# Groups 2 and 3 of the attention output by seven block products, summed up in DRAM

## The chip, the cores and the metric

The kernel runs on one core of a Trainium2 chip. The metric is device time in microseconds of one launch: 727.54 us, the median of three runs (727.34 to 727.63). The profiled execution took 727.55 us, of which its trace spans 725.8 us; 1.75 us lie around the span.

## The reference

Two branches of one input `x` (2048 tokens by 640), mixed by a gate. All of it is float32.

```python
def _A_ref(x, wqkv, wo):                       # 32 heads of 20
    q, k, v = ...                              # x @ wqkv
    pq, pk = phi(q), phi(k)                    # where(t > 0, t + 1, exp(t)) + 1e-6
    kv = einsum("bhsd,bhse->bhde", pk, v)
    z = einsum("bhsd->bhd", pk)
    num, den = einsum("bhqd,bhde->bhqe", pq, kv), einsum("bhqd,bhd->bhq", pq, z) + 1e-6
    return (num / den) @ wo
def _B_ref(x, w_gate, w_up, w_down):
    return (sigmoid(x @ w_gate) * (x @ w_up)) @ w_down
g = sigmoid((x * gate_w).sum(-1))
return g * _A_ref(x) + (1 - g) * _B_ref(x)
```

## The kernel before

Everything is kept transposed, with features in the 128 partitions and tokens in the free dimension. The 640 features are five rows of 128 (`KC`, index k for inputs, o for outputs), the 2048 tokens four groups of 512 (`TG`, index g), the 1536 hidden features of B twelve blocks f.

**Stages.** First k, v and `kv`, then `M`, which is `kv` times `wo`, so that A's last part is one 640 by 640 matrix `M` times p, where p is phi(q). Then q and B for groups 2 and 3 (`f_phase(1, ...)`), then q and B for groups 0 and 1 (`f_phase(0, ...)`, called the f phase below), and the last stage: for each group `out = M (p * fac) + (1 - g) B`, where `fac` is the gate over the denominator. B of groups 2 and 3, already times `1 - g`, waits in `b_dram`; p waits in `p_dram`; `M` is made in DRAM (`m_dram`) and kept there as high and low halves (`mp_dram`). B of groups 0 and 1 is in the SBUF tile `tb`.

**Products.** A float32 product is made of three matmuls in the format float32r, of high and low halves (`mm3`, lines 407 to 409): high by high, high by low, low by high. `split` makes the halves: ACT copies the high one (line 420), DVE subtracts it to get the low one (line 424). One term of one output tile of 128 by 512 is therefore three matmuls.

**Seven products.** Most stages replace the eight products of a 2 by 2 block matrix product by seven (`Block`, steps `s1` to `s7`), with forms S (sums of blocks of the weights) and T (sums of blocks of the inputs) that must be made and split first. Before the change the last stage did so for groups 0 and 1 (`ABlock`: rows 0 and 1, rows 2 and 3 of the output; the fifth input row k = 4 and the fifth output row o = 4 are added plainly by `a_unit`). Groups 2 and 3 were done plainly: ten output tiles of five terms, `a_start` for the first two (line 2611) and `a_unit` for the others. B was put into PSUM ahead of the products (`seed_b`), and each tile went from PSUM to `out_t`.

**What sets the order.** The program is written out by a planner, class `Order`. It keeps estimated clocks for TensorE, ACT and DVE; work that nothing forces yet waits in lists (`urgent`, `items`, `lazy`, `chain`, `spare`) and `fill` places an item as soon as it fits into the slack behind TensorE and its data is thought to have arrived. `need(key)` forces an item. Hooks such as `(FC - 1, 4)` run something after step 4 of block f = 11. Each engine then runs its instructions strictly in the order written.

**Queues and buffers.** Loads go through SP's queue, stores and adding transfers (`accum_op`) through POOL's (GpSimd's). Each queue uses eight semaphores in turn, so a transfer is not issued before the one eight places ahead of it has landed. Tiles come from rotating pools: `ct` gives five buffers of 128 by 512 (`c`), `tt` four (`t`), `x2_tile` ten of twice that size, `h_tile` the `hf` tiles. A tile's next user waits for the last reader of the one before, a transfer too.

In the f phase, `queue_dens` makes `fac` for two groups at a time (five loads of p, ten operations, three small turns through DRAM), and `load_form` and `load_wf` fetch the weights of the blocks ahead: `wg`, `wu`, `ws` (plain and S forms of gate and up), `wf` (those of down).

Of the kernel before, what the change touches and what calls it, by code (L numbers as in the profile page):

```python
# [374 lines left out]
def gated_mix_kernel(ctx: ExitStack, tc: tile.TileContext, xt, xn, wk, wv, wo, wst_q, wst_f, out_t):  # L375
# [1048 lines left out]

    def queue_dens(*gs2):
# [20 lines left out]
        def turn_in(g):  # L1446
            for j in range(4):
                js = slice(j * H, (j + 1) * H)
                sp.dma_start(fac[js, g].rearrange("h (d c) -> h d c", c=P),
                                  den_dram[:, g, j * P:(j + 1) * P].rearrange("(d h) c -> h d c", h=H))  # L1450
            st[g, "gs"] = tt("gs")[:, :P]
            sp.dma_start(st[g, "gs"], gate_rep[4 * g:4 * g + 4].rearrange("i h c -> (i h) c"))
            st["at", g, KC + 1] = lambda: max(order.when(fac[:, g]), order.when(st[g, "gs"])) + 2.5
# [12 lines left out]
        def turn_out(g):  # L1466
            for d in range(4):
                sp.dma_start(fac[d * H:(d + 1) * H, g].rearrange("h (j c) -> h j c", c=P),
                                  fac_dram[:, g].rearrange("(j h) c -> h j c", h=H))
        order.add(0, 0, lambda: [load(g, u) for u in range(2) for g in gs2], chain=True)  # L1470
# [3 lines left out]
        for n, (v, fn) in enumerate(((0, turn_in), (2.0, factor), (0, turn_out))):  # L1474
            for g in gs2:
                order.add(0, v, lambda g=g, fn=fn: fn(g), ("fac", g) if n == 2 else None,
                          lambda g=g, n=n: st.get(("at", g, KC + n), lambda: 1e9)(), **{"first" if n else "chain": True})
# [238 lines left out]
    def queue_m(u=0):  # L1716
# [4 lines left out]
        def fn():  # L1721
# [3 lines left out]
            def rest():  # L1725
                gp.dma_start(mp_dram[:, u], f32(t))
                if u + 1 < KC:
                    queue_m(u + 1)
            order.then(rest)
        order.add(a_cost(D), v_cost(D), fn, "m", lambda: order.when(raw) + 2, spare=True)  # L1730

# [160 lines left out]
    def down_pair(pr, p):  # L1892
# [26 lines left out]
        def far(key, o, g):  # L1919
# [3 lines left out]
            elif not far_at:  # L1923
                far_at.extend(down_pool[1].tile([P, D], F32, name="far", tag=n) for n in ("mr", "mv"))
                far_at.append(down_pool[1].tile([P, TG], F32, name="far", tag="far"))
# [210 lines left out]
    dens = ({3: (2, 3), 7: (0, 1)}, {})  # L2136
# [11 lines left out]
    def f_phase(pr, q, hooks={}):  # L2148
# [70 lines left out]
        for f in range(FC):  # L2219
            if f % 2:  # L2220
                order.need(("h", f // 2 - 1, "B22"), False)
            down = iter(())
            if f in dens[pr]:
                queue_dens(*dens[pr][f])
            if f % 2 and f > 1:
                if pr:
                    pass
                elif f == FC - 1:
                    while any(it[3] == "m" for it in order.spare) or order.pend:
                        order.need("m")  # L2230
                        order._flush()
# [159 lines left out]
    def load_p(g):  # L2391

        PL[g], PL[g, "t"] = [], []
        for u in range(0, KC, 2):
            t = (x2_tile if g == groups[1] else h_tile)(dt=F32)
# [5 lines left out]

    def load_b(g):

        if g < 2:
            BL[g] = [tb[:, o, g] for o in range(KC)]
        elif g == groups[0]:
            BL[g] = [ct("bl") for _ in range(KC)]
            for o in range(KC):
                sp.dma_start(BL[g][o], b_dram[:, o, g - 2])
        else:  # L2410
            t = [x3_tile("bl") for _ in range(2)]
            sp.dma_start(t[0], b_dram[:, 0:3, g - 2])
            sp.dma_start(t[1][:, 0:2], b_dram[:, 3:5, g - 2])
            BL[g] = [t[o // 3][:, o % 3] for o in range(KC)]
# [11 lines left out]
    def pq_tiles(g):  # L2426
# [8 lines left out]
        elif groups.index(g) % 2 == 0:  # L2435
            t = [x2_tile("pq", F32R) for _ in range(5)]
            PQ[g, "t"] = [t[0:3:2], t[1:4:2]]
        else:
            t2 = [x2_tile("pq", F32R) for _ in range(2)]
            t3 = [x3_tile("pq", F32R) for _ in range(2)]  # L2440
            PQ[g] = [tuple(t[:, u] for t in t2) for u in range(2)] + [tuple(t[:, u] for t in t3) for u in range(3)]
            return
# [29 lines left out]
    PT, MS, MR = {}, {}, {}  # L2472

    def load_ms(i):

        if i == 0:
            t = f32(down_pool[1].tile([P, 2, D], F32R, name="mt", tag="mt"))
            raw = [t[:, j] for j in range(2)]
        else:
            raw = [down_pool[1].tile([P, D], F32, name=n, tag=n) for n in ("mr", "mv")]  # L2480
        for j in range(2):
            c0 = (2 * i + j) * P
            m_rows(raw[j].rearrange("p (k c) -> p k c", c=P), slice(c0, c0 + P), gp if i else sp)
        MR[i] = raw, lambda: max(order.when(t) for t in raw)

    def queue_ms(i):

        raw, at = MR.pop(i)
        w = 2 * P
        g, v = raw  # L2490
        a11, a12, a21, a22 = g[:, :w], g[:, w:2 * w], v[:, :w], v[:, w:2 * w]
        g5, v5 = g[:, 2 * w:], v[:, 2 * w:]

        def sums(part):
            if part == 0:
                add(a22, a21, a22)
                sub(a21, a11, a21)
            else:
                sub(a11, a22, a11)
                sub(a12, a12, a11)  # L2500
                sub(g5, g5, v5)

        def form(n, src):
            if i not in MS:
                t = ws_tile() if i == 0 else None
                MS[i] = [t[:, c] for c in range(2)] if t is not None else \
                    [wg_tile().rearrange("p a b -> p (a b)")[:, :9 * P] for _ in range(2)]
            h, l = (t[:, n * w:n * w + width(src)] for t in MS[i])
            split(h, l, src)
        for part in range(2):  # L2510
            order.add(0, 2 * v_cost(w), lambda part=part: sums(part), None, at)
        for n, t in enumerate((a22, a11, a21, a12, g5)):
            order.add(a_cost(width(t)), v_cost(width(t)), lambda n=n, t=t: form(n, t), ("ms", i))

    def queue_pt():
# [5 lines left out]
        def form(t):  # L2521
            if t == 1:
                f = [[down_pool[2].tile([P, TG], F32R, name="pt", tag="c2", bufs=4) for _ in range(2)]
                     for _ in range(2)]
                PT[t] = f
# [4 lines left out]
            PT[t] = [[u[:, j] for u in f] for j in range(2)]  # L2530
# [23 lines left out]
    def a_fifth():  # L2554
# [5 lines left out]
        (2, 7): [queue_m],  # L2560
# [5 lines left out]
        (FC - 1, 4): [lambda: load_ms(0), a_first],  # L2566
# [4 lines left out]
    def next_p():  # L2571
        load_p(groups[1])
        for g in groups[:2]:
            load_b(g)
    last_pair(0, tail, next_p)
    for u in range(KC):
        order.need(("ph", u))
    queue_lo()
    load_ms(1)
    pq_tiles(groups[1])  # L2580
    queue_scale(groups[1])
    queue_pq(groups[1])
    load_p(groups[2])
    load_p(groups[3])

    SEED = {}
    TAGS = ("cc", "ch", "dd", "rot", "rot", "dd", "cc", "ch", "rot", "dd", "cc")

    def seed_b(g, o, tag):

        SEED[g, o] = ps = ps_tile(tag)
        if g < 2:
            vec2(ps, BL[g][o], OMG[g], OP.mult)
        else:
            act(ps, BL[g][o], AF.Copy)

    def queue_seed(g, o, tag, first=True):
        order.add(*((0, v_cost(TG)) if g < 2 else (a_cost(TG), 0)), lambda: seed_b(g, o, tag), ("b", g, o), lambda: BL[g, "at"](), first=first)

    def a_start(units):  # L2600

        ps = [ps_tile(tag) for _, _, tag in units]

        def terms(i, j, first):
            for n, (g, o, _) in enumerate(units):
                os_ = slice(o * P, (o + 1) * P)
                for k in range(KC):
                    l, r = MHL[k, i][:, os_], PQ[g][k][j]
                    if j and n == 0:
                        order.need(("pl", k))  # L2610
                    nc.tensor.matmul(ps[n], l, r, start=first and k == 0, stop=j == 1 and k == KC - 1, skip_group_check=True)  # L2611
                    order.mm(ps[n], TG, first and k == 0, l, r)
                order.fill()
                if j:
                    order.need(("b", g, o))
# [193 lines left out]
```

## Time and profile before

| | |
|---|---|
| median of three runs | 727.54 us |
| profiled execution, its span | 727.55 us, 725.8 us |
| TensorE busy | 721.5 us, 3557 matmuls |
| DVE busy, ACT busy, POOL busy | 573.7 us, 369.0 us, 101.2 us |
| DMA | 182.99 MB, 252 GB/s over the span |
| last stage, from its first matmul to the last operation | 656.69 to 725.8 us |

Matmuls are pipelined: each row of the timeline shows 0.39 us, but the next one starts 0.23 us later. So a sum of TensorE time is made from starts, not from durations. Times in the timeline count from the start of the span. PE in a row is TensorE, SPq is SP issuing a transfer.

### The profile page before, as it was taken

The page shows a single profiled execution, that of the slowest core. Times are in us where ns is not written, and L with a number is a line of the kernel's source. Part 1 is how long each engine was busy: PE and PEld are TensorE (multiplying, and loading weights), DVE is VectorE, ACT ScalarE, POOL GpSimd, SP SyncE. Part 2 cuts the span into 40 slices and gives each one's busy share as a digit, 9 for nine tenths or more (in the row PEclk, how much of TensorE's full clock was granted, in tenths as well). Part 3 has the DMA queues.
Part 4 walks back from the last instruction along what each step waited for, and adds up shares of the span by engine and source line. Part 5 has one row for each costly group of instructions (what it writes and reads, how often), then busy time and mean ns, then how long its engine had stood idle before and what let it go on. Part 6 is the DMA issues. An engine that isn't in the chain of part 4 may idle for free.

```text
span 725.8 us, 10201 instructions
## 1 busy us (share of the span) xinstructions
PE 721.5 (99%) x3557; PEld 619.8 (85%) x3557; DVE 573.7 (79%) x1008; ACT 369.0 (51%) x686; POOL 101.2 (14%) x165
## 2 busy tenths in 40 slices
PE   9999999999999999999999999999999999999998
PEld 8999999988888888888888888888888888888886
DVE  6898878988687889898989954447685868698896
ACT  6884749357656653535454763454333232453551
POOL 0211112113212211211210133000000000012000
PEclk9999999999999999999999999999999999999999
DMA  7676679598787866566787889879979694969612
GB/s 263 156 236 175 178 199 281 134 337 304 262 313 260 330 234 232 180 224 253 254 321 268 245 322 385 322 235 307 327 226 357 207 344 139 359 218 286 249 61 102
DMA packets 79114, 182.99 MB, mean 252 GB/s; under 512 B 12202, under 2 KB 38970, under 8 KB 75478
## 3 DMA queue, kind: packets, MB, share of 16 engines
q1 hardware_dynamic: 60838, 116.94, 49.8%
q0 software_dynamic: 18080, 65.23, 25.8%
q8 instruction: 28, 0.46, 0.3%
q14 instruction: 24, 0.20, 0.1%
q10 hardware_dynamic: 144, 0.16, 0.1%
HBM read 108.68 MB, written 67.07 MB: 242 GB/s over the span
## 4 chain that ended last, share of the span: by engine, by line
PE 99%; DVE 0%; issue 0%
PE ch L407 11%; PE ch L408 11%; PE ch L409 11%; PE cc L407 9%; PE cc L408 9%; PE cc L409 9%; PE dd L407 7%; PE dd L408 7%; PE dd L409 7%; PE rot L408 5%; PE rot L407 5%; PE rot L409 5%; PE rot L1549 1%; PE rot L495 0%; PE ch L2611 0%; PE cc L2611 0%
## 5 line engine op out<-in xcount | busy, mean ns | idle before, releaser
L420 ACT ACTIVATE c<-ch 128x512 f32<-128x512 f32 x52 | 31.1, 598 | 84.0 <-PE ch L409 83.8
L424 DVE TENSOR_TENSOR hf<-c,hf 128x512 fp32r<-128x512 f32 x80 | 54.4, 686 | 22.9 <-ACT hf L420 22.5
L420 ACT ACTIVATE hf<-c 128x512 fp32r<-128x512 f32 x80 | 49.0, 625 | 29.3 <-DVE c L424 29.1
L424 DVE TENSOR_TENSOR c<-cc,c 128x512 f32<-128x512 f32 x40 | 27.6, 689 | 39.0 <-PE cc L409 23.5
L407 PE MATMUL ch<-xth,ws 128*128 128x512 f32 x112 | 43.7, 390 | 0.0
L409 PE MATMUL ch<-xth,ws 128*128 128x512 f32 x112 | 43.6, 389 | 0.0
L408 PE MATMUL ch<-xtl,ws 128*128 128x512 f32 x112 | 43.6, 389 | 0.0
L424 DVE TENSOR_TENSOR tb<-rot,tb 128x512 f32<-128x512 f32 (+1 forms) x58 | 37.0, 672 | 2.8 <-PE rot L409 2.8
L424 DVE TENSOR_TENSOR c<-c,c 128x512 f32<-128x512 f32 x52 | 35.7, 687 | 3.3 <-ACT c L420 2.7
L420 ACT ACTIVATE c<-dd 128x512 f32<-128x512 f32 x22 | 13.1, 597 | 43.5 <-PE dd L409 43.5
L407 PE MATMUL dd<-xrh,wg 128*128 128x512 f32 x90 | 35.2, 391 | 0.0
L409 PE MATMUL dd<-xrh,wg 128*128 128x512 f32 x90 | 35.0, 389 | 0.0
L408 PE MATMUL dd<-xrl,wg 128*128 128x512 f32 x90 | 35.0, 389 | 0.0
L407 PE MATMUL cc<-xbh,ws 128*128 128x512 f32 x84 | 32.7, 389 | 0.0
L408 PE MATMUL cc<-xbl,ws 128*128 128x512 f32 x84 | 32.7, 389 | 0.0
L409 PE MATMUL cc<-xbh,ws 128*128 128x512 f32 x84 | 32.7, 389 | 0.0
L424 DVE TENSOR_TENSOR tb<-dd,tb 128x512 f32<-128x512 f32 x36 | 24.7, 686 | 8.5 <-PE dd L409 8.4
L420 ACT ACTIVATE dd<-ch 128x512 f32<-128x512 f32 x22 | 12.8, 582 | 33.7 <-PE ch L409 33.7
L424 DVE TENSOR_TENSOR wst<-wst 128x256 f32<-128x256 f32 (+1 forms) x65 | 24.6, 396 | 1.4
L424 DVE TENSOR_TENSOR tb<-cc,tb 128x512 f32<-128x512 f32 x36 | 24.4, 683 | 1.2 <-PE cc L409 1.2
L409 PEld LDWEIGHTS ch<-xth,ws 128*128 128x128 f32 x112 | 21.0, 188 | 4.7 <-DVE ws L424 0.2
L420 ACT ACTIVATE c<-c 128x512 f32<-128x512 f32 x34 | 21.3, 628 | 6.9 <-DVE c L424 6.4
(664 smaller groups left out, 2363.5 us busy)
## 6 DMA issues: line engine op xcount, KB each, us to landing
wf<-ws POOLq DMA_DIRECT2D x12, 1152.0 KB, 7.4
ws<-wf SPq DMA_DIRECT2D x11, 1152.0 KB, 8.0
wst<-wst_f SPq DMA_DIRECT2D x12, 640.0 KB, 5.0
wf<-wg POOLq DMA_DIRECT2D x12, 640.0 KB, 6.4
wd<-wd POOLq DMA_DIRECT2D x12, 640.0 KB, 7.9
wg<-wf SPq DMA_DIRECT2D x12, 640.0 KB, 5.6
wf<-wd SPq DMA_DIRECT2D x10, 640.0 KB, 9.5
xnst<-xn SPq DMA_DIRECT2D x16, 320.0 KB, 4.5
```

The source lines that it names most:

```text
L407: nc.tensor.matmul(out, l_hi, r_hi, start=first, stop=False, skip_group_check=True)
L408: nc.tensor.matmul(out, l_hi, r_lo, start=False, stop=False, skip_group_check=True)
L409: nc.tensor.matmul(out, l_lo, r_hi, start=False, stop=last, skip_group_check=True)
L420: nc.scalar.activation(out, src, fn, **kw)
L424: nc.vector.tensor_tensor(out, a, b, op=op)
L1549: nc.tensor.matmul(ps[:w, :w], v[:, m, :w], gt[:, m, c0:c0 + w], start=(m == 0), stop=(m == KC - 1))
```

## The change

Groups 2 and 3 are now done in seven products too.

- The S forms of `M` are made in the f phase for both blocks (`queue_msf`, behind `queue_m`, now from block 3 on), split and stored to a new `ms_dram`; the last stage loads them and makes none.
- The T forms of groups 2 and 3 are made in the f phase without the split (`queue_tp`): p is loaded again, scaled by `fac`, subtracted and stored to a new `pt_dram`. For that all four `fac` are made early (`dens` at blocks 2 and 3, before 3 and 7). The last stage loads and splits the sums (`load_pt`, `queue_form`), and loads three of the five rows of p for group 3 (`load_p3`).
- `a_start` does the products of group 2 that share its p: for both blocks the first two terms and the last three, and the fifth output row. Class `First` does steps 3, 4, 5, 7, 6 for the two blocks alternately; `a_fifth_row` does the fifth row of group 3 on top of what `a_start` left.
- The results aren't seeded with B. Each is summed in a `c` tile and added by POOL's queue into `b_dram`, where B is (`accumulate`). In the last block of products, five transfers bring groups 2 and 3 from `b_dram` to `out_t`.
- The loads of p for group 2 (`load_p0`) come later: after steps 3, 6 and 7 of block 10, before after step 4 of block 9 and steps 3 and 7 of block 10.

```diff
-    dens = ({3: (2, 3), 7: (0, 1)}, {})
+    dens = ({2: (2, 3), 3: (0, 1)}, {})
...
+    def queue_tp(j):
+        src = ((2, j), (2, 2 + j), (3, j), (3, 2 + j))
...
+        def total(n):
+            b11, b21, b12, b22 = raw
+            out, a, b, m = ((b11, b12, b11, 0), (b12, b22, b12, 2), (b22, b22, b11, 1), (b21, b21, b22, 3))[n]
+            sub(out, a, b)
+            gp.dma_start(pt_dram[:, m, j], out)
...
         (FC - 2, 2): [lambda: load_wd(FC - 2)],
-        (FC - 3, 4): [lambda: load_p0(0, 2)],
-        (FC - 2, 3): [lambda: load_p0(2, 4)],
+        (FC - 2, 3): [lambda: order.need('tp'), lambda: load_p0(0, 2)],
+        (FC - 2, 6): [lambda: load_p0(2, 4)],
...
+    def accumulate(g, o, t):
+        gp.dma_start(b_dram[:, o, g - 2], t, accum_op=OP.add)
+
+    def a_start(blks):
...
+        d0, fifth, d1, rest = (ps_tile(t) for t in ("ch", "ch", "dd", "dd"))
+        first, later = range(2), range(2, KC)
+        parts = [(blk.ch, blk.m, first) for blk in blks]
+        parts += [(d0, blks[0].m, later), (fifth, w, first), (d1, blks[1].m, later), (rest, w, later)]
...
+                if n in (0, 1, 3):
+                    out[n] = ct("c11")
+                    act(out[n], ps, AF.Copy, "p")
+                else:
+                    g, o = ((0, 0), (1, 2), (3, 4))[(2, 4, 5).index(n)]
+                    add(out[g], ps, out[g], "p")
+                    accumulate(2, o, out[g])
...
+    class First(ABlock):
...
+        def s4(self):
+            order.need(("pf", 0))
+            order.need(("pq", 3, 4))
+            self.cc = ps_tile("rot")
+            prod(self.cc, self.xt(2, 0, 0) + [self.xb(1, 2, 4)], True)
+            self.c22 = ct("c22")
+            act(self.c22, self.cc, AF.Copy, "p")
+
+        def s5(self):
+            order.need(("pf", 2))
+            prod(self.ch, self.xt(2, 4, 2), False)
+            add(self.c22, self.ch, self.c22, "p")
+            accumulate(3, self.o[1], self.c22)
+
+        def s7(self):
+            for k in range(2, 4):
+                order.need(("pq", 3, k))
+            prod(self.cc, [self.xb(2, 6 + j, 2 + j) for j in range(2)] + [self.xb(2, 8, 4)], False)
+            add(self.c12, self.cc, self.c12, "p")
+            accumulate(3, self.o[0], self.c12)
...
+        if (i, s) == (0, 3):
+            for o in range(KC):
+                sp.dma_start(out_t[o * P:(o + 1) * P, 2 * TG:], b_dram[:, o].rearrange("p g c -> p (g c)"))
```

What this does to the written order, at three places.

**TensorE, the start of the last stage.** `cc`, `ch`, `dd` are PSUM tiles, `pq` the halves of p, `ws` and `wf` those of `M`. Before:

```order
L2611 MATMUL cc_6354<-pq,wf 128x512 x3
L2611 MATMUL ch_6355<-pq,ws 128x512 x2
L2611 MATMUL ch_6355<-pq,wf 128x512 x3
L2611 MATMUL cc_6354<-pq,ws 128x512
L2611 MATMUL cc_6354<-pq,wf 128x512 x4
L2611 MATMUL ch_6355<-pq,ws 128x512
```

Now:

```order
L2700 MATMUL cc_6426<-pq,ws 128x512 x3
L2700 MATMUL cc_6426<-pq,wf 128x512
L2700 MATMUL cc_6427<-pq,ws 128x512 x3
L2700 MATMUL cc_6427<-pq,wf 128x512
L2700 MATMUL ch_6428<-pq,wf 128x512 x6
L2700 MATMUL ch_6429<-pq,ws 128x512 x3
L2700 MATMUL ch_6429<-pq,wf 128x512
L2700 MATMUL dd_6430<-pq,wf 128x512 x6
L2700 MATMUL dd_6431<-pq,wf 128x512 x6
```

The first eight matmuls use rows 0 and 1 of p, the next six (`ch_6428`) rows 2, 3 and 4, two matmuls each. The high halves are used in 30 matmuls, the low ones in the 15 that follow. In all there are 138 matmuls up to `a_unit(0, 4)`, the plain fifth row of group 0, where there were 150.

**ACT, the middle of the last stage**, in the changed program (`c` is a `ct` tile, `rot_6533` and `rot_6547` the products of step 4, `p` the halves of p for group 3, `pt` the fourth T form, `pq` the halves for groups 1 and 0):

```order
L420 ACTIVATE c_6511<-cc_6426 128x512
L420 ACTIVATE p_6304<-hf 128x512
L420 ACTIVATE c_6524<-cc_6427 128x512
L420 ACTIVATE p_6304<-hf 128x512
L420 ACTIVATE c_6543<-rot_6533 128x512
L420 ACTIVATE pt<-pt 128x512 x2
L420 ACTIVATE c_6557<-rot_6547 128x512
L420 ACTIVATE c_6618<-cc_6426 128x512
L420 ACTIVATE pq<-hf 128x512 x3
L420 ACTIVATE c_6635<-cc_6427 128x512
```

Before, ACT put B into PSUM and copied results out of it here, between copies of p. `c_6543` is the eighth tile taken from the five buffers of `ct` (the two `far` tiles are the first two); it gets the buffer of the third, `c_6478`, the first result of `a_start`, and so waits until that one's adding transfer has landed. On DVE the two subtractions for the `pt` copies behind it are the first of 18 operations (the others scale rows of p of groups 0 and 1, add up four results and put B into two PSUM tiles); after these come ten low halves, five of group 1 and then five of group 0.

**SP, the loads for block 9.** Before (`pden` are the rows of p for `fac`):

```order
L364 DMA pden<-p_dram 128x512 x9
L364 DMA wu<-wf_3521 128x768
L364 DMA pden<-p_dram 128x512
L364 DMA wg<-wf_3706 128x1280
L364 DMA ws<-wf_3596 128x2304
L364 DMA wf<-wd_3475 128x2x640 x2
L364 DMA wf<-wd_3475 128x2x1024
```

Now (`mr` and `mv` are the columns of `M` for the first S forms, the `pt` rows those of p for the first T sums):

```order
L364 DMA pt<-p_dram 128x512 x4
L364 DMA wu<-wf_3523 128x768
L364 DMA wg<-wf_3708 128x1280
L364 DMA mr<-m_dram 32x5x128 x4
L364 DMA mv<-m_dram 32x5x128 x4
L364 DMA ws<-wf_3598 128x2304
L364 DMA wf<-wd_3477 128x2x640 x2
L364 DMA wf<-wd_3477 128x2x1024
```

Ten loads of p are gone from here (all `fac` are now made from blocks 2 and 3 on), four others came, and eight transfers of `M`'s columns stand between `wg` and `ws`. The same eight, for the second S forms, stand ahead of `ws` and `wf` of block 11.

More of the change, by code (lines that the diff above doesn't have):

```diff
@@ L2470, in finish @@
         sp.dma_start(out_t[o * P:(o + 1) * P, g * TG + c0:g * TG + c1], dst[:, c0:c1])
[L2472 to L2513, printed above, removed]
+    PT = {}
     def queue_pt():
@@ L2711, in s3 @@
         def s3(self):
-            order.need(("ms", self.i))
             order.need(("pt", 1))
```

295 lines of the change are left out of this document (199 added, 96 removed).

## The prediction

> **What bounds the kernel now.** I read the table of engines on the page first, then the chain of waits, then TensorE's timeline in the last stage.
>
> ```profile
> PE 721.5 (99%) x3557; PEld 619.8 (85%) x3557; DVE 573.7 (79%) x1008; ACT 369.0 (51%) x686; POOL 101.2 (14%) x165
> ```
>
> ```profile
> PE 99%; DVE 0%; issue 0%
> ```
>
> TensorE is busy for 99% of the span and the chain lies on it for the same share. So a matmul that is left out is worth its own time, as long as nothing makes TensorE wait, and every new wait of TensorE counts in full. The price of a matmul comes from the starts of the last stage's first one and of the first one after groups 2 and 3 (a row of x2 is two matmuls):
>
> ```profile
> 656.69 0.62 PE L2611 MATMUL cc<-pq,ws 128*128 128x512 f32 x2
> ...
> 690.69 0.39 PE L407 MATMUL cc<-pq,ws 128*128 128x512 f32 x1
> ```
>
> Between them lie 150 matmuls (ten tiles, five terms, three each) in 34.00 us, 0.2267 us each, with no gap.
>
> **The matmuls taken away.** In the order, groups 2 and 3 now take 45 matmuls in `a_start`, 12 + 18 + 12 + 18 + 18 in steps 3, 4, 5, 7, 6 of both blocks, and 15 in the fifth row: 138. Twelve fewer at 0.2267 us are 2.72 us. Nothing else on TensorE differs. From the profiled 727.55 us (0.01 above the median of the runs, so no correction) the sum starts at 724.83 us, the time if everything else is hidden.
>
> **The start of the last stage: +0.42 us.** `a_start` wants the high halves of rows 3 and 4 of p at its 11th and 13th matmul, since only eight matmuls use rows 0 and 1 and two use row 2. The loads of these rows come later than before, and in the order their two scalings by `fac` now stand on DVE behind the last two additions into `tb` of the f phase; before, the last of them was done at 636.80.
>
> ```profile
> 636.80 0.68 DVE L428 SCALAR_TENSOR_TENSOR wu<-wu,fac 128x512 f32<-128x512 f32 x1
> ...
> 656.73 1.28 DVE L424 TENSOR_TENSOR tb<-rot,tb 128x512 f32<-128x512 f32 x2
> 657.92 2.49 DVE L424 TENSOR_TENSOR pq<-pl,pq 128x512 fp32r<-128x512 f32 x4
> ...
> 684.86 3.09 DVE L424 TENSOR_TENSOR pq<-hf,pq 128x512 fp32r<-128x512 f32 x5
> ```
>
> ```profile
> 637.51 0.63 ACT L420 ACTIVATE pq<-wu 128x512 fp32r<-128x512 f32 x1 [1.07 <-DVE wu L428]
> ...
> 654.23 1.26 ACT L420 ACTIVATE rot<-ch 128x512 f32<-128x512 f32 x2 [2.50 <-PE ch L409]
> ```
>
> Five operations of DVE take 3.09 us and four 2.49, so the starts are 0.60 apart and one alone ends after 0.68. DVE comes free at 657.92, and the scalings end at 658.60 and 659.20. ACT follows 0.03 us after DVE (636.80 + 0.68 against 637.51) and takes 0.60 in a row, which makes the halves ready at 659.23 and 659.83. TensorE wants row 3 at 656.69 + 10 × 0.2267 = 658.96 and waits 0.27; it then wants row 4 at 659.68 and waits 0.15. The bounds are 0.3 us, if DVE comes free 0.1 sooner, and 1.0, if one more operation of 0.60 goes ahead. Rows 0 to 2 are copied by ACT after 654.23 + 1.26 = 655.49 and need 1.8 us, while row 2 is wanted at 656.69 + 8 × 0.2267 = 658.50: no wait. Sum: 725.25 us.
>
> **The wait for the first adding transfer: +0.7 us.** This is the new wait with the most behind it. ACT's copy into `c_6543` waits until `c_6478` has been added into `b_dram`. That transfer is issued when DVE's addition of d0 is done: the first pass of `a_start` ends at 656.69 + 0.42 + 30 × 0.2267 = 663.91, d0 is complete seven matmuls later at 665.50, and the addition ends 0.8 us on, at 666.3; POOL has nothing else to do there, so I put the issue at 666.4. Call the landing L. Behind the copy on ACT's queue stand the two `pt` copies, on which the first of 18 DVE operations wait, and behind these on DVE the ten low halves, of which TensorE first needs the sixth (group 0, row 0). With 0.60 for the copy, 0.60 for the first `pt`, 18 × 0.605 = 10.9 and 6 × 0.605 = 3.6, that half exists at L + 15.7. `a_unit(0, 4)` begins 138 matmuls after the start, at 656.69 + 0.42 + 31.28 = 688.39, and its second matmul wants the half at 688.62. So nothing is lost up to L = 672.8 or so, that is, a transfer of 6.4 us, and each microsecond beyond is lost. (A second way through the same copy, step 7 of the first block at 676.8, allows more.) The trace of before has no adding transfer into DRAM at this place. The nearest rows, with bytes and median from issue to landing:
>
> ```profile
> p_dram<-qe POOLq DMA_DIRECT2D x20, 256.0 KB, 4.7
> zacc<-kr POOLq DMA_DIRECT2D x8, 320.0 KB, 4.5
> b_dram<-tb POOLq DMA_DIRECT2D x10, 256.0 KB, 7.1
> tb<-far POOLq DMA_DIRECT2D x4, 256.0 KB, 10.2
> ```
>
> ```profile
> DMA to landing us min/median/max: 8.3/10.2/12.1
> ```
>
> The last line is for the tile `far`. At 4.5 or 4.7 us nothing is lost, at 7.1 us 0.7, at 10.2 us 3.8, at the longest of 12.1 us 5.7. These are the bounds, 0 and 5.7. I take 7.1: the same destination, size and queue. The `far` rows add too, but were issued inside a stretch in which SP loads the biggest weights, while by 666 those have landed. Sum: 725.95 us.
>
> What bears on the value is how busy the DMA engines are here (columns: us, PE, PEld, DVE, ACT, POOL busy with counts, clock, DMA share, GB/s):
>
> ```profile
> 650.00:660.00 10.00, 10.00 (x46) 8.29 (x45) 9.95 (x17) 2.81 (x6) 4.07 (x7) 1.00 1.06 289
> 660.00:670.00 10.00, 10.00 (x46) 8.29 (x45) 8.92 (x15) 4.50 (x9) 2.84 (x6) 1.00 1.06 281
> 670.00:680.00 10.00, 10.00 (x45) 8.29 (x45) 6.15 (x10) 3.80 (x7) 0.00 (x0) 1.00 1.05 392
> ```
>
> They are full from 650 to 680 already, and the change loads more here, about 1.8 MB of S forms and 2.1 MB of T sums, against less p and no B for groups 2 and 3.
>
> [...]
>
> **Weights of the f phase: 0, at most +2.0 us.** SP's queue now issues eight columns of `M` ahead of `ws` and `wf` of block 9, and again for block 11. Before:
>
> ```profile
> 573.39 0.42 SPq L364 DMA_DIRECT2D wg<-wf  x1
> ...
> 574.97 1.92 SPq L364 DMA_DIRECT2D wf<-wd  x3
> ```
>
> ```profile
> wf<-wd SPq DMA_DIRECT2D x2, 640.0 KB, 10.7
> ...
> wg<-wf SPq DMA_DIRECT2D x1, 640.0 KB, 5.2
> ```
>
> ```profile
> 586.65 0.39 PE L407 MATMUL ch<-xth,ws 128*128 128x512 f32 x1
> ...
> 588.01 0.39 PE L407 MATMUL dd<-hf,wf 128*128 128x512 f32 x1
> ```
>
> `wf`, issued at 574.97, landed 10.7 us later, at 585.7, and was first used at 588.01: 2.3 us of room. Now `ws` is the ninth transfer behind `wg` with eight semaphores, so it is not issued before the first column has landed. That one goes out at about 573.8, behind `wg`; by `wg`'s 5.2 us it lands at 579, and `ws` and `wf` go 4.4 us later than before. If their transfers take as long as before, TensorE waits for `wf` from 588.0 to 590.0: +2.0. If 1.15 MB of `ws` and 0.64 MB of `wf` arrive by themselves at the 390 GB/s of 670 to 680, they take 4.6 us and land at 584: 0. I take 0, because ten loads of p that stood ahead of `wg` are gone, so that the queue comes to this place emptier. In block 11 the room is of the same kind, and the same answer serves.
>
> **Work that is hidden.** DVE and ACT get the T sums (8 scalings and 8 subtractions, 16 × 0.605 = 9.7 us of DVE) and, moved from the last stage, the S forms (about 3.6 us of DVE for each block by these rows):
>
> ```profile
> 694.94 2.00 DVE L424 TENSOR_TENSOR mt<-mt 128x256 f32<-128x256 f32 x5
> 696.86 1.62 DVE L424 TENSOR_TENSOR ws<-mt,ws 128x256 fp32r<-128x256 f32 x5
> ```
>
> ```profile
> 570.00:640.00 70.00, 70.00 (x311) 57.86 (x310) 51.05 (x83) 24.48 (x45) 2.16 (x4) 1.00 0.83 267
> ```
>
> DVE was idle for 19 us of these 70, and the order puts the new items singly behind TensorE's blocks, so 17 us fit; without that cover they would be paid in full. The additions of `fac` only move from blocks 3 and 7 to 2 and 3. In the last stage DVE loses the S forms between 691 and 710, where 16.31 of 17 us were busy, so the tail can only get easier:
>
> ```profile
> 691.00:708.00 17.00, 17.00 (x77) 14.08 (x76) 16.31 (x29) 10.02 (x19) 0.00 (x0) 1.00 0.17 62
> ...
> 722.36 0.42 DVE L424 TENSOR_TENSOR tb<-rot,tb 128x256 f32<-128x256 f32 x1 [1.37 <-PE rot L409]
> ```
>
> The end after the last matmul stays as it is. The five transfers from `b_dram` to `out_t`, 2.62 MB, run from about 700 on with the DMA engines at 0.17; at the 281 GB/s of 660 to 670 they need 9.3 us and are done well before 722. The loads of `pt` and `ms`, finally: SP's stretch begins at the row below, and at the 289 GB/s of 650 to 660 the 2.24 MB of `mp`, 1.77 MB of `ms` and the first two pairs of T sums (1.05 MB) take 17.5 us, to 660; POOL's share of the traffic may make that 664, and the first `pt` copy on ACT is wanted at about 665.5.
>
> ```profile
> 642.60 0.33 SPq L364 DMA_DIRECT2D wf<-mp_dram  x1
> ```
>
> Cost 0; with the cover gone (3 us later) TensorE would wait about 1.5 us at step 3.
>
> **The rivals.**
>
> *The adding transfer lands after 6.5 to 10 us.* Full DMA engines speak for it, the 4.5 us of `zacc` against it. TensorE then stands at `a_unit(0, 4)` by the excess over 6.4 us, and most or all of the gain goes: 726.1 to 729.0 us.
>
> *The adding transfer is as slow as the `far` rows.* [...] At 10.2 us the loss is 3.8 us (729.05), at 12.1 us 5.7 (731.0). It decides for slower from 10.2 us on. Against it: the additions into `zacc` are bigger and took 4.5 us.
>
> *The weights of block 9 or 11 come late.* Up to 2.0 us of waiting at steps that use `wf`: 727.25 without the wait for the transfer, 727.95 with it, no change. For it speaks the eight-semaphore queue; against it the ten loads that are gone.
>
> *The copies in DRAM at the end hold up the last outputs*, or `pt` is late by more than 3 us. Against both stand the shares above; 729 or more if either is so.
>
> That the change does not do what it says is excluded for the matmuls, which the order counts.
>
> **How the numbers follow.** This kernel's measurement tells 0.2%, 1.46 us, from no change: faster is below 726.1, slower above 729.0. The forecast (L within about 7.2 us of its issue, weights in time) has 0.46, with a range of its own from 724.6 to 726.1 and 725.95 as its time. A transfer of 7.2 to 10.1 us has 0.19, one slower than that 0.18, late weights 0.13, the end or the T sums 0.04. Hence faster 0.46, no change 0.32, slower 0.22. The range from 724.6 to 729.3 leaves out some 0.15 of slower cases and 0.03 below.
>
> **What would show it.** TensorE x3545 and DVE x1026. In TensorE's timeline gaps of 0.27 and 0.15 us at the 11th and 13th matmul of the last stage, released by ACT; a gap ahead of the fifth row of group 0, released by DVE, as long as the transfer of `c_6478` exceeds 6.4 us, and an idle time of ACT ahead of `c_6543` that ends with POOL's queue. No gap at 588 or 625. I am wrong if TensorE stops in the f phase, if step 3, 4, 5 or 6 waits for a `pt` tile, or if the row of `b_dram<-c` shows 4 us and TensorE stops there all the same.

## The result, and the profile after

The changed kernel takes 733.01 us (median of four runs, 731.76 to 734.26), the one before 727.59 us on the same chip. The ratio is 1.0074, with a 95% interval of 1.0056 to 1.0092: 5.4 us slower, where 725.95 us was predicted and 729.3 was the range's end. The execution whose trace is read here is the longest of its four, and of the kernel with the last stage alone, further down, one execution of ten took 1468.64 us and is left out of the median.

The profiled execution took 734.26 us. Its table of engines and its chain of waits:

```profile
PE 721.8 (99%) x3545; PEld 617.1 (84%) x3545; DVE 588.2 (80%) x1026; ACT 370.0 (51%) x682; POOL 111.4 (15%) x180
...
PE 85%; DMA 9%; DVE 3%; SPq 1%; ACT 1%; issue 1%; ACTq 0%; DVEq 0%
```

The matmuls are the 3545 that the order counted, but the chain now runs for 9% of the span through transfers, where it had none. (The busy share hardly shows this: 721.8 of 732.6 us and 721.5 of 725.8 us both print as 99%. So the chain and the starts are what to read.) The waits are counted here as the time between the starts of neighbouring matmuls beyond 0.2267 us, which has no excess in the kernel before from 440 us on; in the changed one it adds up to 8.51 us:

| place | beyond 0.2267 us per matmul | what TensorE waits for |
|---|---|---|
| block 5, 513 to 522 us | 5.30 | `ws`, `wf` of down (twice) |
| block 9, 594 us | 0.44 | `wf` |
| block 11, 630 to 634 us | 0.92 | `ws`, `wf` |
| `a_start`, rows 3 and 4 of p | 0.63 | ACT's high halves |
| fifth row of group 0, 696 us | 1.23 | DVE's low half |

Less 2.72 us for the twelve matmuls, that makes +5.8 us; the two profiled executions differ by 6.7. Of the other 0.9, 0.54 us is there by 9.6 us from the start, in stages that the change does not touch: the first matmuls start 0.43 us apart in both executions, and come to 0.15 us at 6.3 us here, at 5.5 us in the kernel before. The rest I leave unexplained.

Five eighths of the waiting is in block 5, which the prediction never speaks of. Its matmuls with a wait, in TensorE's timeline:

```profile
515.63 0.50 PE L407 MATMUL ch<-xth,ws 128*128 128x512 f32 x1 [1.79 <-DMA ws<-wf]
...
518.54 0.50 PE L407 MATMUL dd<-hf,wf 128*128 128x512 f32 x1 [1.26 <-DMA wf<-wd]
...
522.36 0.47 PE L407 MATMUL dd<-hf,wf 128*128 128x512 f32 x1 [1.46 <-DMA wf<-wd]
```

What SP did there, first in the kernel before, then in the changed one (start, time until the last of the row was issued, count):

```profile
499.07 0.32 SPq L364 DMA_DIRECT2D wg<-wf  x1
501.11 0.32 SPq L364 DMA_DIRECT2D ws<-wf  x1
501.48 2.62 SPq L364 DMA_DIRECT2D wf<-wd  x3
```

```profile
499.15 1.74 SPq L364 DMA_DIRECT2D fac<-den_dram  x4
500.94 0.43 SPq L364 DMA_DIRECT2D gs<-gate_rep  x1
501.46 0.85 SPq L364 DMA_DIRECT2D pden<-p_dram  x2
503.05 0.32 SPq L364 DMA_DIRECT2D wg<-wf  x1
503.46 1.81 SPq L364 DMA_DIRECT2D fac<-den_dram  x4
505.32 0.43 SPq L364 DMA_DIRECT2D gs<-gate_rep  x1
505.85 0.38 SPq L364 DMA_DIRECT2D pden<-p_dram  x1
506.32 0.38 SPq L364 DMA_DIRECT2D ws<-wf  x1
509.66 1.72 SPq L364 DMA_DIRECT2D mr<-m_dram  x4
511.42 1.84 SPq L364 DMA_DIRECT2D wf<-wd  x3
```

`ws` goes out 5.2 us later and `wf` 9.9 us later. Two moves of the change meet here. `fac` of groups 0 and 1 is made from block 3 on, so that ten more rows of p and the turns share SP's queue with the weights. And `queue_m` is hooked behind block 3 instead of block 2; the hook runs just ahead of `load_wf`, which puts the four loads of `mr` in front of `wf`. The first `mr` is eight transfers behind `wg` and goes out when that has landed (509.58, issued 509.66); in both traces SP's transfers go out at least 0.02 us after the landing of the one eight places ahead, wherever that landing is recorded.

The DMA engines were not full all the while. The windows of before and after, with the DMA share and GB/s last:

```profile
480.00:500.00 20.00, 20.00 (x89) 16.54 (x89) 13.94 (x22) 12.42 (x22) 1.08 (x2) 1.00 0.88 281
...
510.00:530.00 20.00, 20.00 (x90) 16.52 (x89) 13.39 (x22) 6.77 (x12) 1.08 (x2) 1.00 0.91 312
```

```profile
480.00:500.00 20.00, 20.00 (x90) 16.52 (x89) 15.37 (x26) 10.94 (x20) 1.08 (x2) 1.00 0.64 207
...
510.00:530.00 20.00, 15.49 (x66) 11.84 (x66) 13.33 (x23) 6.11 (x11) 1.61 (x3) 1.00 1.04 369
```

First they idle more than before, then everything comes at once.

For `ws` the two can be told apart. In the kernel before, TensorE wants it 12.0 us after its issue (501.11 to 513.16), and it lands after 8.3. In the changed one TensorE wants it 7.4 us after its issue (506.32 to 513.69), and starts with it after 9.3 (515.63). So the transfer is 1 us slower; but with the 12.0 us of before it would still have been in time.

### The profile page after: what moved, and what is told of

The parts are those of the page before. It is cut to its first block, busy times and chain, and to the rows that moved or that the text cites. A ratio compares the mean times of both kernels' runs of the same rounds, so it can differ in the third digit from the quotient of the medians.

```text
span 732.6 us, 10285 instructions
## 1 busy us (share of the span) xinstructions
PE 721.8 (99%) x3545; PEld 617.1 (84%) x3545; DVE 588.2 (80%) x1026; ACT 370.0 (51%) x682; POOL 111.4 (15%) x180
## 4 chain that ended last, share of the span: by engine, by line
PE 85%; DMA 9%; DVE 3%; SPq 1%; ACT 1%; issue 1%; ACTq 0%; DVEq 0%
PE ch L407 9%; PE ch L408 9%; PE ch L409 9%; PE cc L407 8%; PE cc L408 8%; PE cc L409 8%; PE dd L407 6%; PE dd L408 6%; PE dd L409 6%; PE rot L408 5%; PE rot L407 5%; PE rot L409 5%; DMA wu<-wf 2%; DMA wf<-wd 2%; DMA mr<-m_dram 2%; DMA ws<-wf 1%
## 5 line engine op out<-in xcount | busy, mean ns | idle before, releaser
L407 PEld LDWEIGHTS ch<-xth,ws 128*128 128x128 f32 x112 | 21.0, 188 | 7.1 <-DMA ws<-wf 3.0
L409 PEld LDWEIGHTS ch<-xth,ws 128*128 128x128 f32 x112 | 21.0, 188 | 4.7 <-DVE ws L424 0.2
```

The source lines that it names most:

```text
L407: nc.tensor.matmul(out, l_hi, r_hi, start=first, stop=False, skip_group_check=True)
L409: nc.tensor.matmul(out, l_lo, r_hi, start=False, stop=last, skip_group_check=True)
```

## The experiments

The theory: SP issues strictly in order, as its rows for block 9 of the changed kernel show (`wg` at 578.48 us, the eight columns from 579.33, `ws` at 586.41), and what now stands ahead of `ws` and `wf` makes the weights of block 5 late ("queue"). The rivals: the DMA engines are full whichever queue asks ("bytes"); or the loss is in the last stage or in the T sums.

**One part of the change alone: `fac` early, in the kernel before.**

```diff
-    dens = ({3: (2, 3), 7: (0, 1)}, {})
+    dens = ({2: (2, 3), 3: (0, 1)}, {})
```

> The kernel before, with one line of the change: fac of all four groups is started at blocks 2 and 3 instead of 3 and 7. Nothing of the last stage is changed, so there are 3557 matmuls. In the order the ten loads of p for groups 0 and 1 and both sets of turns now stand on SP's queue ahead of ws and wf of block 5. Queue theory (SP issues strictly in order, and loads of p that wait for DVE hold up the weights behind them): TensorE waits in block 5 for ws and wf, 3 to 6 us in all, 730.5 to 733.5 us. Rival, the rest of the change (columns of M from block 3 on, T sums, S forms) makes the wait in block 5: no wait here, 727.5 us.

Measured 739.84 us, ratio 1.0171 (1.0154 to 1.0188). The wait is there, larger than expected, and for a reason of its own:

```profile
507.27 11.64 SPq L364 DMA_DIRECT2D pden<-p_dram  x4
518.97 1.18 SPq L364 DMA_DIRECT2D wf<-wd  x2
```

```profile
523.28 0.79 PE L407 MATMUL dd<-hf,wf 128*128 128x512 f32 x1 [8.62 <-DMA wf<-wd]
```

SP stands for 11.6 us with rows of p in front of `wf`. Here the tile `gs` still takes one of the four `tt` buffers until DVE has used it (the last of two such uses ends at 518.57, the fourth row goes out at 518.59). After the stop TensorE runs at half its rate until 527.3 us, which costs 2.0 us more (the granted clock of this execution is 0.992, in the kernel before 1.000; the page has the digit 7 for it from 515.6 to 534.0 us and 9 everywhere else; the last section has more on this). The change gives `gs` a tile of its own and puts the way in of the turns into another of the planner's lists, so this size is not the change's; the mechanism is.

**The other part alone: `queue_m` behind block 3, in the kernel before.**

```diff
-        (2, 7): [queue_m],
+        (3, 7): [queue_m],
```

> The kernel before, with one line of the change: the columns of M start behind block 3 instead of block 2, which puts four of them between ws and wf of block 5 on SP. No other part of the change. As in the run with fac at blocks 3 and 7, TensorE waits 1.9 us for wf there: 729.5 us. If that wait came from something else of the change: 727.6 us.

733.04 us, ratio 1.0074 (1.0059 to 1.0090): this one line costs as much as the whole change loses in the net. The execution with the trace is the shortest of its four (731.78) and has 3.34 us of waiting in block 5 and 0.68 in block 7. Its queue:

```profile
501.24 0.32 SPq L364 DMA_DIRECT2D ws<-wf  x1
501.66 2.08 SPq L364 DMA_DIRECT2D mr<-m_dram  x4
503.85 6.48 SPq L364 DMA_DIRECT2D fac<-den_dram  x4
510.37 0.43 SPq L364 DMA_DIRECT2D gs<-gate_rep  x1
510.84 2.82 SPq L364 DMA_DIRECT2D wf<-wd  x3
```

`ws` is in time. `wf` goes out 9.4 us late, since the four columns push the turn of `fac` in front of it, and this spends 6.5 us. The expectation had the place right and half the size.

**The change with `fac` as before.**

```diff
-    dens = ({2: (2, 3), 3: (0, 1)}, {})
+    dens = ({3: (2, 3), 7: (0, 1)}, {})
...
-            if not pr and f == 4:
+            if not pr and f == 8:
                 for j in range(2):
                     queue_tp(j)
```

> The changed kernel with fac made at blocks 3 and 7 as before, and the T sums queued at block 8 (they need all four fac). SP's order of the loads of block 5 is then word for word that of before. Queue theory: the waits of block 5 (5.3 us) are gone, 733.0 - 5.3 = 727.7 us, plus what it costs that all eight loads of p for the T sums now come behind the weights of block 11 (0 to 3 us). Rival, more bytes on the DMA engines throughout the f phase: half or more of the 5.3 us stays, 730.5 us or more.

759.93 us, ratio 1.044. In block 5 the wait falls from 5.30 to 1.91 us. It is not zero, since the hook stays (the expectation took SP's order there for that of before, which it is not: the columns still stand ahead of `wf`). The rest of the loss is a new one: the T sums are forced at one place, and DVE waits there for their rows, once for 9.6 us:

```profile
628.89 2.68 DVE L428 SCALAR_TENSOR_TENSOR pt<-pt,fac 128x512 f32<-128x512 f32 x4 [9.63 <-DMA pt<-p_dram]
```

TensorE stands for 25.3 us. This is the price of the T sums without their cover, which the prediction had put at their 9.7 us of DVE: the loads' latency counts too.

**The same loads from POOL's queue.**

```diff
-                sp.dma_start(st[g, u], p_dram[:, u, g])
+                gp.dma_start(st[g, u], p_dram[:, u, g])
```

(and so for the turns and `gs` in `queue_dens`)

> The changed kernel, with every load that queue_dens makes (p, the two turns, the gate sums) issued from POOL's queue instead of SP's; the same bytes at about the same time. Four columns of M still stand ahead of wf of block 5 on SP. Queue theory: ws of block 5 comes in time, at most 1 us of wait for wf is left there, the waits of blocks 9 and 11 (1.3 us) and of the last stage (1.9 us) stay: 727.5 to 729 us. Rival, bytes (the DMA engines are full there, whichever queue asks): the waits stay, 732 to 733 us. Rival, the columns of M ahead of wf are the cause of its part: 1.95 us of the wait for ws go and 3.3 us of those for wf stay, 731 us.

In block 5 the wait falls from 5.30 to 0.76 us, as the queue theory has it, with the same bytes. (Block 5 comes 5 us later here, since TensorE stops at 492 us; but `ws`, too, goes out later, at 506.53, and is wanted at 518.58, 12.0 us on as in the kernel before.) The time is still 737.11 us, ratio 1.0132. At 492 us DVE waits for a row of p through POOL (4.2 us), and TensorE for DVE, which with the slow matmuls after it costs 5.55 us, the most in this run; `ws` and `wf` of block 7 come late by 3.2 us in all, `wf` of block 9 by 1.0. The wait moved with the transfers.

**Rows of p or turns?** Six of the ten rows for `fac` of groups 0 and 1 are left out:

```diff
             if u < KC:
-                st[g, u] = tt("pden")
+                ... (for g < 2 and u > 1: the tile of row u - 2 again, no load)
```

> The changed kernel with six of the ten loads of p for fac of groups 0 and 1 left out (the same four rows are used again, so fac of these groups is wrong); DVE's work, the turns and the columns of M stay. On SP the three rows ahead of wg and ws of block 5 are gone. Theory of the rows (SP waits with them for DVE to free a buffer, and the weights wait behind): the wait of block 5 falls from 5.3 to that of the columns of M alone, 1.5 to 2 us; 729.5 to 730 us. Rival, the ten small loads of the turns hold up the weights: 4 us or more of it stay, 732 us or more.

731.33 us, ratio 1.0053 (1.0038 to 1.0068). Block 5 falls to 0.66 us, although the turns and the columns stay where they were:

```profile
501.17 0.38 SPq L364 DMA_DIRECT2D wg<-wf  x1
501.65 1.80 SPq L364 DMA_DIRECT2D fac<-den_dram  x4
503.49 0.43 SPq L364 DMA_DIRECT2D gs<-gate_rep  x1
504.02 0.38 SPq L364 DMA_DIRECT2D ws<-wf  x1
504.50 3.45 SPq L364 DMA_DIRECT2D mr<-m_dram  x4
508.00 1.84 SPq L364 DMA_DIRECT2D wf<-wd  x3
```

With `ws` 2.3 and `wf` 3.4 us sooner than in the change, the weights are nearly in time. So the rows of p weigh most. But blocks 7 and 9 now wait 1.3 and 1.2 us (in the change 0 and 0.4), block 11 0.9 as there, and the total is above what was expected for that reason.

**Turns and columns on POOL, against the same kernel with them on SP.** Both put `queue_m` back behind block 2, start the T sums when `fac` of groups 2 and 3 is there, and have the two edits of the last stage that are shown further down.

```diff
-                sp.dma_start(fac[js, g]..., den_dram...)
+                gp.dma_start(fac[js, g]..., den_dram...)
```

(and so for the way out, `gs` and the columns in `queue_msf`; the kernel on SP has none of these)

> The changed kernel with the columns of M from block 2 on, the T sums started once fac of groups 2 and 3 is there (they need no other), and the two edits of the last stage (buffer, start). The turns of fac and the S forms' columns stay on SP's queue: ten turn loads and three rows of p stand ahead of ws and wf of block 5. Queue theory: 3 to 5 us of waiting in block 5, some in others, 728 to 731 us.

> As the run before, but the turns of fac (small loads between DRAM and SBUF) and the S forms' columns are issued from POOL's queue; same work, same bytes. Queue theory (what counts is what stands ahead of ws and wf on SP): the wait in block 5 falls below 1 us, none in blocks 9 and 11, 725 to 727 us, faster than the kernel before. Rival (the DMA engines are full, so the weights come late whichever queue asks): within 1 us of the run before.

737.35 and 737.25 us: no difference, and here the queue theory fails as it was put. In block 5 the one on SP waits 3.90 us, the one on POOL 3.07; in block 7 they wait 1.2 and 2.2, and the one on POOL 1.8 more in block 9. On POOL's version SP issues

```profile
499.06 1.44 SPq L364 DMA_DIRECT2D pden<-p_dram  x3
500.55 0.42 SPq L364 DMA_DIRECT2D wg<-wf  x1
501.49 2.92 SPq L364 DMA_DIRECT2D mr<-m_dram  x4
504.51 0.76 SPq L364 DMA_DIRECT2D ws<-wf  x1
505.31 4.10 SPq L364 DMA_DIRECT2D wf<-wd  x3
```

so rows of p and the columns of `queue_m` still stand ahead of `ws`, which is 3.4 us later than before, and it lands 11.7 us after its issue (516.24), where before it took 8.3. Both count: when a load is issued, and how long it is under way. `wf`, issued only 3.8 us late, costs next to nothing. The equal totals say little on the queue, since each kernel loses some 4 us more at another place: the one on SP 4.2 us at and after a stop for DVE at the end of the f phase (657 to 665 us), the one on POOL 4.1 us at and after a stop for ACT and DVE at the fifth row of group 0 (696 to 702 us). At both places TensorE then runs at half its rate for some 3 us (the granted clock is 0.998 over each of the two executions, 1.000 in the kernel before).

**The last stage by itself.** `fac` and `queue_m` as before, no T sums (rows of p are loaded in their place):

```diff
-                for j in range(2):
-                    queue_tp(j)
+                pass
...
-            sp.dma_start(f32(f[j][1]), pt_dram[:, t, j])
+            sp.dma_start(f32(f[j][1]), p_dram[:, 2 * (t % 2) + j, 2 + t // 2])
```

> The new last stage with an f phase close to that of before: fac at blocks 3 and 7, the columns of M from block 2 on, and no T sums (left out; where the last stage would load them it loads rows of p of the same size, so T is computed with other data). The S forms are made as in the change. If all that the change loses lies in the f phase's loads: 727.6 - 2.72 + 0.63 (start of the stage) + 1.23 (adding transfer) = 726.7 us, and up to 1.3 more if the S forms' columns still hold up the weights of blocks 9 and 11. If the last stage itself is slower than its matmuls say: 728 us or more.

727.68 us (median of nine), ratio 1.0001 (0.9991 to 1.0010). Block 5 has no wait; `ws` goes out at 501.24 and `wf` at 501.61. What is left is 2.10 us in block 7, where the columns for the S forms now stand ahead of `wf` (issued at 548.81, in the kernel before at 538.20), and 0.80 at the fifth row of group 0; `a_start` has none. That is 2.9 us, which eats the 2.72 of the matmuls.

**The buffer of step 4.** From that kernel, one edit:

```diff
-            self.c22 = ct("c22")
+            self.c22 = tt("c22")
             act(self.c22, self.cc, AF.Copy, "p")
```

> As the run with the new last stage and fac as before (no T sums), with one edit: step 4's copy takes a buffer of another pool, so that it waits for no adding transfer; the orders of DVE and TensorE stay the same. Theory of the buffer: ACT's wait ahead of step 4's copy and TensorE's 0.80 us at the fifth row of group 0 are gone; the time falls by 0.8, to 727.0 us. Rival, DVE's work as a whole sets that wait: 0.4 us or more of it stays.

726.85 us, 0.8 below the run before, ratio 0.9992 (0.9980 to 1.0005) to the kernel before. The executions lie between 725.60 and 729.58 us, so the traces carry this reading; all engines have the same order in both runs. In the changed kernel ACT's row, and TensorE's at the fifth row, read

```profile
681.71 0.60 ACT L420 ACTIVATE c<-rot 128x512 f32<-128x512 f32 x1 [0.92 <-DMA b_dram<-c]
...
697.43 0.50 PE L408 MATMUL ch<-pq,ws 128*128 128x512 f32 x1 [0.95 <-DVE pq L424]
```

in the run before

```profile
675.46 0.60 ACT L420 ACTIVATE c<-rot 128x512 f32<-128x512 f32 x1 [0.83 <-DMA b_dram<-c]
...
691.18 0.50 PE L408 MATMUL ch<-pq,ws 128*128 128x512 f32 x1 [0.53 <-DVE pq L424]
```

and in this one, followed by TensorE at the fifth row,

```profile
675.09 0.58 ACT L420 ACTIVATE c<-rot 128x512 f32<-128x512 f32 x1
```

```profile
690.84 0.39 PE L407 MATMUL ch<-pq,ws 128*128 128x512 f32 x1
691.06 0.39 PE L408 MATMUL ch<-pq,ws 128*128 128x512 f32 x1
```

Neither waits. From the transfer to TensorE, the chain of the prediction is shown. All that this kernel waits for from 440 us on is 2.20 us in block 7. Without that it would stand near 724.7 us by the median, 725.6 by the execution with the trace (727.79): 2 to 3 us below the kernel before, where the matmuls give 2.72. This is an estimate; that version was not built, and it has no T sums.

**Three edits at once.** The buffer, the fifth row's first two terms ahead of rows 2 to 4 in `a_start`, and the S forms' columns on POOL's queue:

```diff
-        parts += [(d0, blks[0].m, later), (fifth, w, first), (d1, blks[1].m, later), (rest, w, later)]
+        parts += [(fifth, w, first), (d0, blks[0].m, later), (d1, blks[1].m, later), (rest, w, later)]
...
-                m_rows(raw[j].rearrange("p (k c) -> p k c", c=P), slice(c0, c0 + P), sp)
+                m_rows(raw[j].rearrange("p (k c) -> p k c", c=P), slice(c0, c0 + P), gp)
```

> As the run before, with three edits: step 4's copy takes a buffer that no adding transfer reads, a_start does the fifth row's first two terms ahead of rows 2 to 4, and the S forms' columns are loaded through POOL's queue. If the three waits have the causes named, none is left: 727.6 - 2.72 = 724.9 us (724.5 to 725.5), about 1.9 to 3 below the run before. If a wait of the last stage comes from DVE's load as a whole and not from the transfer: 726 us or more.

730.88 us, ratio 1.0041: six us above what was expected. Blocks 7 and 9 wait 0.9 and 1.7 us, and the fifth row of group 0 1.8, more than with the transfer's wait. The planner, given other times, put DVE's addition of step 5's product ahead of the low halves of the fourth T form, and DVE stands with it until TensorE gets there:

```profile
678.47 0.69 DVE L424 TENSOR_TENSOR c<-cc,c 128x512 f32<-128x512 f32 x1 [1.85 <-PE cc L409]
```

The same edits, with everything of `queue_dens` and the T sums' loads on POOL's queue too:

```diff
-                sp.dma_start(raw[-1], p_dram[:, u, g])
+                gp.dma_start(raw[-1], p_dram[:, u, g])
```

> As the run with the loads of fac on POOL's queue; besides, the columns of M for the S forms and the rows of p for the T sums go through POOL's queue, the copy of step 4's result takes a buffer that no adding transfer reads, and a_start does the fifth row's first two terms ahead of the terms of rows 2 to 4. If all four waits (block 5, blocks 9 and 11, the start of the last stage, the adding transfer) have the causes named, none is left: 727.55 - 2.72 = 724.8 us, 724.5 to 726. If full DMA engines make those of the f phase: 729 us or more.

748.30 us, ratio 1.028. TensorE waits for weights, for DVE and for ACT all over the f phase and at its end. Each move gave the planner other times, and it wrote another order with other waits.

**The change without the T sums.**

```diff
-                for j in range(2):
-                    queue_tp(j)
+                pass
```

(and the last stage loads rows of p, as above)

> The changed kernel without the T sums: nothing is scaled, summed or stored for them, and the last stage loads rows of p of the same size in their place (T is computed with other data). SP's order up to block 8 is that of the change. If the T sums are hidden, as the prediction had it, the waits of block 5 (5.3 us) and of the last stage stay: 732 to 733 us, at most 1.3 less for blocks 9 and 11. If their 16 DVE operations and 4 MB of transfers cost time themselves: 731 us or less.

730.48 us, ratio 1.0037 (1.0022 to 1.0052): 2.5 us less than the change, where the prediction had the T sums hidden. In the profiled execution block 5 waits 3.34 us, block 9 0.96, block 11 and `a_start` nothing, the fifth row of group 0 1.10. Block 5 lies ahead of the first T sum, and SP's order is the same there; 5.30 against 3.34 us shows how far its wait varies from one traced execution, of one build, to another, and is no cost of the T sums. The rest, 1.1 us, is at `a_start`, at the fifth row and in blocks 9 and 11 together. Only this speaks against the T sums being hidden, with one trace on each side.

## Why the prediction was wrong

The forecast was faster, 725.95 us; the result is slower. Among the signs of being wrong the prediction named a stop of TensorE in the f phase, and this is the one that came. Step by step:

- **The matmuls** (−2.72 us): right. 3545 of them, and in the kernels with a quiet f phase the gain is there.
- **The start of the last stage** (+0.42): right in place, releaser and nearly in size, 0.63 us. What was left out is that the first two matmuls after each of the two stops start 0.34 us apart, not 0.23 (666.79 to 667.13, 667.39 to 667.73).
- **The first adding transfer** (+0.7 for 7.1 us): right. It was issued at 674.45 and landed at 681.62, 7.17 us; the loss was 1.23 us. In the kernel with the last stage alone it took 6.74 us and cost 0.80: the slope of one to one holds (0.43 us each), and the limit is about 5.9 us instead of 6.4. Four more runs agree when one counts from the issue to the start of ACT's copy: in all six kernels that have this buffer, with 6.83 to 7.46 us between the two, TensorE waits 6.0 us less than that (0.80 to 1.47). The row that was taken as nearest, `b_dram<-tb` with 7.1 us, came very near; that a plain transfer fits an adding one so well is luck, since the ten adding transfers took 4.1 to 9.0 us. The rival by the `far` rows did not come.
- **Weights of blocks 9 and 11** (0, bounds 0 and 2.0): 1.36 us together. The place was right, and the wrong end was taken. The reason given, that ten loads of p are gone from ahead of `wg`, bought little: TensorE is 5.9 us behind the kernel before in block 9, and `wg` goes out 5.1 us later (578.48 against 573.39). And SP needs 7.0 us to issue the eight columns (579.33 to 586.31), which was not counted, so `ws` goes out 6.7 us later behind `wg` than before, where the prediction had 4.4. In the kernel where the columns fell into block 7 they cost 2.10.
- **"The additions of `fac` only move from blocks 3 and 7 to 2 and 3"**: this is the step that failed. It counted DVE's operations and put their cost at nothing because DVE has room. It did not follow the ten loads of p and the turns to the place where they arrive, though the block-9 step had just used their absence there. At the new place they stand on SP ahead of `wg`, `ws` and `wf` of block 5, where TensorE waits 5.30 us in the changed kernel and 0.66 with six of the ten rows left out.
- **`queue_m` behind block 3 instead of 2**: it stood in the diff and was given no price. Alone it costs 5.4 us by the medians; the trace, of its shortest execution, shows 4.0 us of it.
- **The T sums as hidden work**: probably wrong, by 1.1 us in the waits behind them; the 2.5 us of the whole time include block 5, which lies ahead of them. DVE's idle 19 us were the only cover named, and its loads and stores, 4 MB, were not.

The range was built from the waits that were named, and all of these were in the last stage or in blocks 9 and 11. The two moves of the f phase add up to 5.30 us in block 5, while either alone gave 1.9 to 3.9 there (the hook 1.9 and 3.3 in two kernels, `fac` early 3.9 in the kernel with turns on SP; the 8.6 us of the first run belong to `gs`). So they don't simply add, and how the 5.30 us split between the two is left open. Late issue is a condition of the wait for `ws` there (the 12.0 us of before would have covered the 9.3 us of the transfer, and the 11.7 us of the run with turns on POOL); for `wf`, and for the other blocks, late issue and slow landing are not told apart. Moving the rows or leaving them out removed most of block 5's wait, but in all kernels that did so other blocks waited more.

No version that computes everything beat the kernel before. The nearest, the two with the last stage alone and no T sums, are even with it.

## What to carry to other kernels

When work is moved, follow each of its loads to its new place in the queue, count what its issue takes there, and read off which weights stand behind it; a busy share that leaves room on the computing engine says nothing on that. A hook's place decides what its loads stand in front of: here one line that moved four small loads ahead of a weight load cost twice what twelve matmuls gave. And a planner that fills slack by estimated times answers an edit with a new order: compare orders, change one thing at a time, and keep the DVE and TensorE orders fixed in the test, as the buffer's run did.

## What was not expected of the hardware

After some stops TensorE runs slowly for a while. In the run with all of `queue_dens` on POOL's queue:

```profile
496.58 0.80 PE L407 MATMUL rot<-hf,wf 128*128 128x512 f32 x1 [3.82 <-DVE tb L424]
497.18 0.63 PE L408 MATMUL rot<-hf,wf 128*128 128x512 f32 x1
...
499.74 0.40 PE L408 MATMUL cc<-hf,wf 128*128 128x512 f32 x1
499.97 0.40 PE L409 MATMUL cc<-hf,wf 128*128 128x512 f32 x1
```

Matmuls start 0.43 us apart for 2.5 us, then 0.23 again; in the stretch from 492 to 500 us the granted clock is 0.79. It cost 1.6 us beside the stop itself. After the stop of 2.7 us in the run with turns on POOL nothing of the kind is seen (granted clock 1.00 from 510 to 520 us):

```profile
516.29 0.50 PE L407 MATMUL ch<-xth,ws 128*128 128x512 f32 x1 [2.73 <-DMA ws<-wf]
516.62 0.39 PE L408 MATMUL ch<-xtl,ws 128*128 128x512 f32 x1
```

The length of the stop alone does not decide it. In the run with turns on SP the slow rate came about 2 us after the end of a stop of 2.0 us:

```profile
659.77 0.50 PE L407 MATMUL cc<-hf,ds 128*128 128x512 f32 x1 [2.01 <-DVE tb L424]
...
662.22 0.63 PE L408 MATMUL ch<-hf,ds 128*128 128x512 f32 x1
662.65 0.63 PE L409 MATMUL ch<-hf,ds 128*128 128x512 f32 x1
```

The granted clock is 0.79 from 657 to 665 us there, too. The changed kernel, with stops of 1.8 us and less in block 5, shows no slow stretch: after each of them its matmuls start 0.31 to 0.34 us apart once and then 0.22 to 0.24, at a granted clock of 1.00 from 510 to 530 us. What decides is not shown by these runs.
